# A gated recurrence and a spatial-gating block on one core: the state's decay moved into its product, mixing cut into steps, and a new order of steps

## The chip, the cores and the metric

The kernel runs on one core of a Trainium2 chip. Times are device microseconds (us) of one execution, and the profile is one execution recorded by the hardware. TensorE (PE) does the products, PEld is its weight loading, VectorE (DVE), ScalarE (ACT) and GpSimd (POOL) do element-wise work, and SP, ACT and POOL issue transfers.

## What is computed

A matrix-valued recurrence over 768 steps (batch 4, 8 heads of width 40), whose output goes through a gated feed-forward block that mixes over the sequence:

```python
for t in range(S):                                  # attention part
    m_new = maximum(f[t] + m, i[t])
    C = exp(f[t] + m - m_new) * C + exp(i[t] - m_new) * outer(v[t], k[t])
    n = exp(f[t] + m - m_new) * n + exp(i[t] - m_new) * k[t];  m = m_new
    y[t] = sigmoid(o[t]) * (C @ q[t]) / maximum(abs(n . q[t]), 1)
h = relu(x @ w_in); u, v = h[:512], h[512:]         # x is y, 320 wide
v_s = w_spatial @ layernorm(v) + b_spatial          # mixes the 768 positions
out = (u * v_s) @ w_out
```

## The kernel before

**Blocks.** The sequence of each batch is cut into 6 blocks of 128 positions, each of two chunks of 64; 24 blocks n in all, block n being k = n mod 6 of batch b = n div 6. Inside a chunk the recurrence is a masked product; between chunks a state of 40 x 41 per head is carried.

**One attention block.** s (line 605): scores of the two chunks, one in the upper and one in the lower half of the rows. ex (line 608): one product of the tables AT and GM, which hold the gates' running sums, gives the exponents; W (ACT, line 623) is its exponential. In batch 0 a second product eb (line 618) with a table sel gives Eb, the decay along a chunk; in the other batches Eb is loaded. KS takes s times W (DVE, line 629) and q times Eb (POOL, line 637). kt (POOL, line 648) scales k by the last column of W. dc (lines 659, 661) is k times v of each chunk, 64 rows each, the first chunk in rows 0 to 63, the second in rows 64 to 127. The state of the second chunk is dc plus the first state times its decay (d1 line 677, c1 line 680), that of the next block again (d2 line 687, c2 line 690); a block with k = 0 only copies (line 672). The states lie in RH below or above the rows of v, so that pv (lines 702, 703) gives a chunk's own part and the state's part in one product: 104 rows for the first chunk (64 where k = 0, since there is no state yet), 128 for the second. Then den (line 714), two products on DVE (lines 720, 723), a transpose px (line 743), and the split of x into a high and a low part (xH, xL).

**The feed-forward part.** All products of it are done in three terms (high x high, high x low, low x high). Per batch: six V (line 796, tile pm), each followed by the norm on ACT, DVE and POOL (lines 803 to 836) which gives vH and vL; eight pairs of pu (line 856) and pb (lines 862 to 864). A pb is 18 products over all six blocks of V in one accumulation, so it waits for the last of them; then bias, gate and split (lines 873 to 883); six pc (lines 899 to 901) and the output.

**Weights.** They come as 64-bit numbers and are converted on chip in cvt (lines 442 to 490): one ACT step, four DVE steps, a copy to the high part, a subtraction and an addition, in two banks of PSUM. The rest rows of w_in (64 of 320) come as one transfer for both halves.

**The order.** A list written out by hand (ORDER) gives every step's place; each engine and each queue runs its steps in that order. TensorE works in order, and a step that waits holds up all behind it. The loads of blocks, weights and the gate rows of block 0 (GM, lines 414 to 421) go over SP's queue, constant tables over POOL's. PSUM has 8 banks (pool "bank"), and the list's order sets which step gets which.

Of the kernel before, what the change touches and what calls it, by code (L numbers as in the profile page):

```python
# [8 lines left out]
F32 = mybir.dt.float32  # L9
F32R = mybir.dt.float32r  # L10
I32 = mybir.dt.int32
U32 = mybir.dt.uint32
# [13 lines left out]
RW = 2 * VW + 2 * KW  # L26
# [4 lines left out]
NKS, NRH = 3, 3  # L31
DEC_POOL = (0,)
GATE_POOL = (1, 2)
# [17 lines left out]
class Task:  # L51
    def __init__(self, name, eng, cost, fn, mode, lock, size):
        self.name, self.eng, self.cost, self.fn, self.mode, self.lock, self.size = name, eng, cost, fn, mode, lock, size
        self.deps, self.succ, self.bufs = set(), [], []
        self.due = self.own = None

    def length(self):
        return self.cost + (2.0 + self.size / 200.0 if self.size else 0.0)


class Plan:
# [11 lines left out]
    def add(self, name, eng, cost, fn, r=(), w=(), mode="M", lock=False, size=0, due=None, after=(), hold=()):  # L73
        t = Task(name, eng, cost, fn, mode, lock, size)
        t.own = due
        t.deps.update(after)
        for write, group in ((False, r), (True, w)):
            for x in group:
                b, part = x if isinstance(x, tuple) else (x, None)
                for o, p, wr in b.seen:  # L80
                    if o is not t and (write or wr) and (p is None or part is None or p == part):
                        t.deps.add(o)
                if write:
                    b.seen = [s for s in b.seen if part is not None and s[1] != part]
                b.seen.append((t, part, write))
                if b.pool and b not in t.bufs:
                    t.bufs.append(b)
                    b.users += 1
# [3 lines left out]
        for o in t.deps:  # L92
            o.succ.append(t)
# [5 lines left out]
half_neg rhz0 ident i sel f warm qk0_0 cgm0 qk0_1 cat0 rh0_0 cgm1 rh0_1 rhz1 wir_ld wi0 wi10_ld wi11_ld m0 rst rh1_0 m1 ksz2 rh1_1 ksz0 fa1 qk1_0 fs1  # L99
rhz2 qk1_1 fa0 ksz1 g1 s0 cat1 fs0 gh1 g0 eg1 is0 as0 gh0 gl1 ah0 dg0 gl0 da0 dg1 al0 wg1 m2 dg2 da1 dg3 wg0 eg0 fa2 th0 fs2 wa0 g2 gm1 ex0 is1 ebm0  # L100
gh2 rh2_0 W0 gl2 rh2_1 Eb0 as1 ks0_0 ebm1 wir_1 ks0_1 kt0 ah1 wir_2 we1 q0_1 Eb1 dc0 wir_3 wi10_1 c1_0 al1 wir_h0 qk2_0 wi10_2 pv0 qk2_1 is2 wa1 wir_4
wir_h1 den0 d2_0 wir_h2 wi10_3 wi11_1 xm0 as2 wir_h3 wi11_2 ra01 wi11_3 wi10_h0 wi10_4 wi11_h0 wir_s0 q1_0 ah2 wi11_4 gm2 wg2 xg0 q1_1 eg2 wir_5 ex1
rh3_0 th1 rh3_1 wi10_5 s1 W1 al2 wi10_s0 gm3 px0 qk3_0 wir_s1 kt1 wa2 qk3_1 ex2 wi11_5 xh0 we0 xj0 W2 wi11_s0 dc1 th2 wi10_l0 kt2 s2 ra02 wir_l1 ebm2
wi11_l0 Eb2 c2_0 dc2 gm4 xl0 d1_1 th3 xk0 ks1_0 V00 q2_0 ks1_1 c1_1 ks2_0 d2_1 pv1 ks2_1 re00 q2_1 c2_1 sq00 ex3 bsp den1 ebm3 s3 xm1 W3 d1_2 qk5_0
xg1 Eb3 qk5_1 va00 wir_l0 px1 kt3 rh4_0 gm5 rh4_1 c1_2 q3_0 xh1 dc3 ks3_0 xj1 ks3_1 pv2 d2_2 xl1 xk1 ex4 den2 q3_1 ebm4 W4 V01 c2_2 xm2 wi00_ld Eb4
xg2 wi01_ld d1_3 qk4_0 qk4_1 po00 px2 c1_3 re01 rh5_0 pv3 d2_3 nb00 rh5_1 xh2 xj2 ra10 xl2 gm6 th4 kt4 s5 c2_3 sq01 den3 we2 d1_4 xm3 ws00_ld dc4 vh00
xg3 ws01_ld ex5 rh6_0 c1_4 vn00 ebm5 px3 xk2 rh6_1 d2_4 va01 W5 V02 ws02_ld Eb5 ws03_ld po01 c2_4 ws04_ld xh3 ks5_0 d1_5 xj3 ks5_1 wi00_1 q5_0 xl3
re02 xk3 wi00_2 V03 ra11 sq02 gm7 q4_0 nb01 wi00_3 wi01_1 va02 wi00_4 vh01 q4_1 s4 wi01_2 re03 wi01_3 sq03 q5_1 qk6_0 ks4_0 qk6_1 th5 ks4_1 eb6_0 vn01
kt5 qk7_0 va03 pv4 wi01_4 qk7_1 ws00_h po02 eb7_0 wi00_5 ws01_h eb7_1 po03 dc5 wi00_h0 den4 vl00 xm4 ex6 wi01_h0 c1_5 W6 xg4 pv5 vl01 nb02 rh7_0 nb03
vh02 wi01_5 rh7_1 px4 den5 vn02 kt6 ex7 xm5 xh4 xg5 vl02 dc6 xj4 xl4 vh03 xk4 px5 wi00_s0 vn03 V04 ws00_l xh5 ws01_l ws05_ld xj5 ws02_h xl5 vl03  # L110
# [42 lines left out]
def ordered(plan):  # L153
# [816 lines left out]
```

## Time and profile before

| | |
|---|---|
| runs (us) | 424.12, 420.58, 418.35 (median 420.58) |
| profiled execution: span (us) | 422.7 |
| TensorE busy | 369.7 us |
| DVE, ACT, POOL busy | 250.9, 152.5, 139.8 us |
| mean granted clock of TensorE | 0.927 |
| moved | 35.62 MB |

Busy time of TensorE is time in which some product is under way, and products overlap, so a busy share near 100% does not say that it runs at its best. The granted clock is a share of 2.4 GHz. In waits, the releaser is what ended an idle time.

### The profile page before, as it was taken

How to read it: one execution, taken by the hardware profiler on the slowest of the kernel's cores; microseconds unless marked ns; L12 is line 12 of the kernel's file. 1: busy time of each engine (PE TensorE's matmuls, PEld its weight loads, DVE VectorE, ACT ScalarE, POOL GpSimd, SP SyncE). 2: the span in 40 equal slices, each digit the busy share in tenths (PEclk: the TensorE clock that was granted, in tenths of full speed). 3: DMA queues.
4: the chain of work that ended last, by engine and by line, in shares of the span. 5: the costliest groups of instructions: out<-in, count | busy, mean ns of one | idle time of the engine just before them, and what ended most of it. 6: DMA issues, size and time to landing. Idle time of an engine off the chain costs nothing.

```text
span 422.7 us, 9190 instructions
## 1 busy us (share of the span) xinstructions
PE 369.7 (87%) x3654; PEld 335.1 (79%) x3654; DVE 250.9 (59%) x540; ACT 152.5 (36%) x363; POOL 139.8 (33%) x150
## 2 busy tenths in 40 slices
PE   2045996979969999989799989999799999999996
PEld 1023874768869998868699878998699998899995
DVE  6145979867998737569693574335952626434231
ACT  2044268646331205723501521156320408441212
POOL 8044578753350114546530313325440004230000
PEclk9999999677969999989779985999779999999999
DMA  9940569354820505326312073200210100000001
GB/s 166 227 116 12 133 202 223 118 139 118 213 75 18 158 30 143 102 79 154 101 46 73 7 185 92 85 16 24 72 47 2 33 16 2 33 16 2 16 33 47
DMA packets 17262, 35.62 MB, mean 84 GB/s; under 512 B 3960, under 2 KB 9196, under 8 KB 17220
## 3 DMA queue, kind: packets, MB, share of 16 engines
q1 hardware_dynamic: 12556, 29.72, 26.6%
q10 hardware_dynamic: 4136, 4.52, 3.3%
q0 software_dynamic: 528, 0.81, 1.2%
q8 instruction: 29, 0.48, 0.5%
q14 instruction: 13, 0.11, 0.1%
HBM read 30.59 MB, written 4.42 MB: 83 GB/s over the span
## 4 chain that ended last, share of the span: by engine, by line
PE 67%; DVE 14%; DMA 10%; issue 4%; ACT 3%; POOL 1%; SPq 1%; ACTq 0%; DVEq 0%; POOLq 0%
PE pu L856 9%; PE pb L862 8%; PE pb L863 8%; PE pb L864 8%; PE pm L796 7%; PE pv L702 5%; DMA QK<-in_qk 5%; PE s L605 5%; PE pv L703 4%; PE pc L899 3%; PE pc L901 3%; PE pc L900 2%; PE dc L659 2%; DMA RH<-in_vk 2%; DVE KS L629 2%
## 5 line engine op out<-in xcount | busy, mean ns | idle before, releaser
L637 POOL TENSOR_TENSOR KS<-QK,Eb 40x512 f32<-40x512 f32 x44 | 57.5, 1312 | 70.1 <-PE pv L703 32.8
L862 PE MATMUL pb<-wsH,vH 128*128 128x384 f32 x192 | 68.0, 354 | 3.9 <-DVE wo_r L468 3.9
L863 PE MATMUL pb<-wsL,vH 128*128 128x384 f32 x192 | 67.1, 350 | 0.0
L864 PE MATMUL pb<-wsH,vL 128*128 128x384 f32 x192 | 66.9, 349 | 0.0
L873 DVE TENSOR_TENSOR pb<-pb,bsp 128x384 f32<-128x384 f32 x32 | 18.1, 565 | 54.3 <-PE pb L864 54.3
L883 ACT CAST gt<-pb 128x384 fp32r<-128x384 f32 x32 | 15.4, 480 | 76.7 <-DVE pb L876 76.7
L703 PE MATMUL pv<-RH,KS 128*64 128x41 f32 x384 | 37.9, 254 | 5.1 <-DVE KS L629 3.2
L702 PE MATMUL pv<-RH,KS 104*64 104x41 f32 (+1 forms) x384 | 38.0, 253 | 4.7 <-DVE KS L629 3.0
L605 PE MATMUL s<-QK 40*64 40x64 f32 x768 | 34.3, 251 | 8.9 <-DMA QK<-in_qk 8.9
L862 PEld LDWEIGHTS pb<-wsH,vH 128*128 128x128 f32 x192 | 38.1, 198 | 4.4 <-DVE wo_r L468 4.2
L605 PEld LDWEIGHTS s<-QK 40*64 40x64 f32 x768 | 30.6, 162 | 13.5 <-DMA QK<-in_qk 9.2
L812 POOL TENSOR_TENSOR st<-st,half_neg 128x1 f32<-128x1 f32 x24 | 13.4, 560 | 82.0 <-DVE st L809 65.8
L702 PEld LDWEIGHTS pv<-RH,KS 104*64 104x64 f32 (+1 forms) x384 | 31.2, 158 | 10.9 <-POOL st L812 3.3
L836 POOL TENSOR_TENSOR vL<-v,vH 128x512 fp32r<-128x512 f32 x24 | 31.1, 1299 | 23.6 <-ACT vH L818 15.2
L863 PEld LDWEIGHTS pb<-wsL,vH 128*128 128x128 f32 x192 | 38.2, 199 | 0.0
L864 PEld LDWEIGHTS pb<-wsH,vL 128*128 128x128 f32 x192 | 38.0, 198 | 0.0
L703 PEld LDWEIGHTS pv<-RH,KS 128*64 128x64 f32 x384 | 31.2, 159 | 7.7 <-DVE KS L629 2.8
L629 DVE TENSOR_TENSOR KS<-s,W 64x512 f32<-64x512 f32 x48 | 32.9, 686 | 6.9 <-PE s L605 4.3
L648 POOL TENSOR_TENSOR RH<-RH,W 128x320 f32<-128x320 f32 x24 | 18.7, 781 | 49.0 <-ACT W L623 34.9
L856 PE MATMUL pu<-xH,wiH 128*128 128x384 f32 x96 | 33.1, 345 | 0.0
L856 PE MATMUL pu<-xH,wiL 128*128 128x384 f32 x96 | 32.6, 340 | 0.0
L796 PE MATMUL pm<-wiH,xH 128*128 128x512 f32 x72 | 31.5, 437 | 0.0
(117 smaller groups left out, 818.8 us busy)
## 6 DMA issues: line engine op xcount, KB each, us to landing
RH<-in_vk SPq DMA_DIRECT2D x48, 242.0 KB
QK<-in_qk SPq DMA_DIRECT2D x48, 160.0 KB
out<-o ACTq DMA_DIRECT2D x24, 160.0 KB
Eb<-scr_e SPq DMA_DIRECT2D x33, 80.0 KB
ws<-in_w_sp SPq DMA_DIRECT2D x12, 192.0 KB
wi_raw<-in_w_in SPq DMA_DIRECT2D x4, 512.0 KB
wo_raw<-in_w_out SPq DMA_DIRECT2D x4, 320.0 KB
wir_raw<-in_w_rem SPq DMA_DIRECT2D x1, 512.0 KB
```

What stands on the lines that cost most here:

```text
L605: self.nc.tensor.matmul(o[64 - p0:128 - p0, h], q[p0:p0 + D, 0, h], q[p0:p0 + D, 1, h], start=True, stop=True)
L629: self.nc.vector.tensor_tensor(out=KS.t[r, e], in0=st()[r], in1=self.T(W)[r], op=ALU.mult)
L637: self.nc.gpsimd.tensor_tensor(out=KS.t[r, e], in0=self.T(QK)[r, 1], in1=self.T(Eb)[r], op=ALU.mult)
L648: self.nc.gpsimd.tensor_tensor(out=kt, in0=kt, in1=self.T(W)[:, :, L - 1:L].broadcast_to([128, H, D]), op=ALU.mult)
L702: self.nc.tensor.matmul(o[0:64, h], ks[0:ke, 0, h], v0[0:ke, h], start=True, stop=True)
L703: self.nc.tensor.matmul(o[64:128, h], ks[:, 1, h], v1[:, h], start=True, stop=True)
L796: self.nc.tensor.matmul(pmt(), l, r, start=i == 0, stop=i == len(terms) - 1)
L836: self.nc.gpsimd.tensor_tensor(out=vl(), in0=vt(), in1=vh().bitcast(F32), op=ALU.subtract)
L856: self.nc.tensor.matmul(put(), w, x, start=i == 0, stop=i == len(terms) - 1)
L862: self.nc.tensor.matmul(pbt(), vH[:, cd], wh[:, s], start=s == 0, stop=False)
L863: self.nc.tensor.matmul(pbt(), vH[:, cd], wl[:, s], start=False, stop=False)
L864: self.nc.tensor.matmul(pbt(), vL[:, cd], wh[:, s], start=False, stop=s == NB - 1)
```

## The change

The state's decay moves into dc. The k part of RH gets, beside the 64 rows of k, 40 to 64 rows of an identity (eye); kt multiplies both at once by the last column of an exponent tile XY that now holds W and Eb side by side, so that the identity becomes diagonal rows with the decay on them. dc then has 104 or 128 rows (k and v in 64 of them, decay and old state in the rest) and gives the new state directly; four heads go to the lower and four to the upper half of the output. It is two steps now, dc_0 and dc_1, and each is followed by two copies (cc), on DVE or ACT, in place of products and additions. For k = 0 the state rows are set to zero (cz), and pv has 104 and 128 rows in every block. In batch 0 the decay comes from a second exponent product with a table ATX, in place of eb.

pb is cut into six steps of three products, one for each block of V, and pc into four, each its own entry in the list. The gate's product is written to u in SBUF, not back to the bank.

Constant tables come from one transfer (const) and are spread out on chip. A conversion of weights has one ACT and three DVE steps in an SBUF tile, a copy and a subtraction. The rest rows of w_in are loaded once per half and twice over (0.5 MB more).

The list is new: it names an engine for steps that can run on more than one (copies, products, transfers), and so moves 27 of the 48 q and 16 of the 24 kt steps to DVE, 20 of 32 gl steps to POOL, and transfers from SP to ACT and POOL. The limits that were built in for the old list (pv of block n-2 ahead of s of block n, and so on) are gone. There are two KS tiles instead of three.

```diff
-NKS, NRH = 3, 3
-POOLS = dict(bank=8, QK=2, Eb=2, big=5, xL=3, xH=3, W=2, tmp=2, x=2, v2=14, s15=4, den=2, st=3, raw=4, late=1)
+NKS, NRH, NXY, NGM = 2, 3, 2, 2
+POOLS = dict(bank=8, QK=2, KT=2, big=5, xL=3, xH=3, x=2, v2=14, s15=4, den=2, st=3, raw=3)
...
-half_neg rhz0 ident i sel f warm qk0_0 cgm0 qk0_1 cat0 rh0_0 cgm1 rh0_1 rhz1 wir_ld wi0 wi10_ld wi11_ld m0 rst rh1_0 m1 ksz2 rh1_1 ksz0 fa1 qk1_0 fs1
-rhz2 qk1_1 fa0 ksz1 g1 s0 cat1 fs0 gh1 g0 eg1 is0 as0 gh0 gl1 ah0 dg0 gl0 da0 dg1 al0 wg1 m2 dg2 da1 dg3 wg0 eg0 fa2 th0 fs2 wa0 g2 gm1 ex0 is1 ebm0
+i@SP axz1@DVE axz0 f@ACT const@ACT cz0 qk0_0 rst axe0 m0 qk0_1 fa0 qk1_1@POOL qk1_0@POOL s0 is0@POOL rh0_1 fs0@POOL m1 g0 as0 gh0 ah0 al0@POOL
+axe1@DVE gmh0 fa1 s1 fs1 da1@ACT wa0@ACT is1@POOL gl0 gmm0 dg0@POOL dg1@ACT g1 rhz1@DVE rh0_0 dg2@POOL dg3@ACT gh1@DVE ksz1 as1 da0 gmm1 gl1 ah1 m2
...
+nb01 vn01 wi02_ld vh01 ws11_ld den4 vl01 re02 vl00@DVE pb001_0 pb000_0 sq02 wi01_3 ws01_h@POOL xg4 wi02_1 ws01_l@POOL ws02_ld xm4 px4 pb003_0 pb001_1
...
-                self.nc.tensor.matmul(o[0:D, h], kt[0:64, h], v0[0:64, h], start=True, stop=True)
-                if not last:
-                    self.nc.tensor.matmul(o[64:64 + D, h], kt[64:128, h], v1[64:128, h], start=True, stop=True)
...
-            add(f"d1_{n}", de, dcost, dec1, r=[(RH, "c0"), (Eb, 1)], w=[t1], lock=True)
-            add(f"c1_{n}", "DVE", 0.42, st1, r=[dc, t1], w=[(RH, "c1")])
...
+        def ktm(e):
+            self.eng(e).tensor_tensor(out=ktt(), in0=self.rh_k(n), in1=xyt()[:, :, :, L - 1:L].broadcast_to([128, 2, H, D]), op=ALU.mult)
...
+        for e in range(1 if last else 2):
+            def dcm(q, e=e):
+                kt, v, o, K = ktt(), self.rh_v(n, e), dct(), (64 + D, 128)[e]
+                for h in range(4):
+                    for p0 in (0, 64):
+                        hh = h + p0 // 16
+                        self.nc.tensor.matmul(o[p0:p0 + D, e, h], kt[0:K, e, hh], v[0:K, hh], start=True, stop=True)
+            def put(q, g, e=e):
+                m = n + e
+                lo = 64 * e
+                self.copy(q, self.rh_v(m, 1 - e)[lo:lo + D, 4 * g:4 * g + 4], dct()[64 * g:64 * g + D, e])
...
-            ke = 64 if k == 0 else 64 + D
...
-                self.nc.tensor.matmul(o[0:64, h], ks[0:ke, 0, h], v0[0:ke, h], start=True, stop=True)
+                self.nc.tensor.matmul(o[0:64, h], ks[0:64 + D, 0, h], v0[0:64 + D, h], start=True, stop=True)
...
-        vs = [x for s in range(NB) for x in self.vn[b, s]]
-        self.pbt.append(add(f"pb{name}", "PE", 3.15, pbm, r=vs + [F(f"wsH{hf}"), F(f"wsL{hf}")], w=[pb], due=self.moe_due(b, "pb", i), hold=[gt]))
...
+        for s in range(NB):
+            add(f"pb{name}_{s}", "PE", lambda e, s=s: pbm(s), r=[*self.vn[b, s], (F(f"wsH{hf}"), s), (F(f"wsL{hf}"), s)], w=[pb])
```

The new conversion of weights, whose steps take the place of shift, sign, power, low, a subtraction and an addition:

```diff
+        add(name + "_1", "ACT", base, r=[rb], w=[y])
+        add(name + "_2", "DVE", shift, w=[y])
+        add(name + "_3", "DVE", sign, r=[rb], w=[y])
+        add(name + "_4", "DVE", tail, r=[rb], w=[y])
+        add(name + "_h", "ACT/POOL", lambda e: self.copy(e, H_(), yt().bitcast(F32)), r=[y], w=[(F(wbuf + "H"), part)])
+        add(name + "_l", "DVE/POOL", lambda e: self.eng(e).tensor_tensor(out=L_(), in0=yt().bitcast(F32), in1=H_().bitcast(F32), op=ALU.subtract),
```

## Rows read from the trace of the kernel before

**Rows 1.** The page, part 1: busy time, share, instructions of each engine.

```profile
PE 369.7 (87%) x3654; PEld 335.1 (79%) x3654; DVE 250.9 (59%) x540; ACT 152.5 (36%) x363; POOL 139.8 (33%) x150
```

**Rows 2.** Busy time by stretch: length, each engine, granted clock, transfer share, GB/s.

```profile
0.00:50.00 50.00, 19.99 (x234) 15.52 (x234) 27.04 (x52) 15.32 (x35) 20.20 (x33) 1.00 0.61 138
50.00:130.00 80.00, 68.92 (x830) 58.37 (x829) 67.53 (x148) 41.68 (x97) 45.94 (x45) 0.85 0.53 144
130.00:410.00 280.00, 272.01 (x2543) 253.22 (x2542) 154.08 (x338) 93.08 (x227) 73.61 (x73) 0.93 0.21 60
410.00:422.70 12.70, 8.79 (x54) 8.00 (x52) 2.25 (x4) 2.42 (x6) 0.00 (x0) 1.00 0.11 39
```

**Rows 3.** Waits of PE: who waited for whom, us, times, longest.

```profile
PE ex L608 <- DMA GM<-gp: 14.8, 1, 14.8
PE s L605 <- DMA QK<-in_qk: 8.9, 3, 5.0
PE ex L608 <- issue: 5.2, 1, 5.2
```

**Rows 4.** Busy time by stretch again: the wait at the start, and around pv18.

```profile
10.00:24.00 14.00, 0.00 (x0) 0.00 (x0) 2.57 (x4) 0.54 (x3) 0.00 (x0) 1.00 0.81 196
249.40:263.00 13.60, 13.33 (x134) 11.65 (x135) 5.84 (x15) 1.55 (x3) 3.32 (x4) 0.52 0.37 104
```

**Rows 5.** Timeline of SP: start, us, engine, line, what it issues.

```profile
12.79 10.29 SPq L418 DMA_DIRECT2D GM<-gp  x4
```

**Rows 6.** Timeline of PE, start of the kernel: start, us, line, tiles, shapes.

```profile
24.71 0.77 PE L608 MATMUL ex<-GM,AT 84*128 84x512 f32 x1 [14.80 <-DMA GM<-gp]
...
41.36 0.76 PE L608 MATMUL ex<-GM,AT 84*128 84x512 f32 x1 [5.23 <-issue]
```

**Rows 7.** Chain of work that ended last, in order of time: the first V.

```profile
50.01 2.96 PE pm L796 x8
```

**Rows 8.** Timeline of PE, 52 to 57 us: a pv of blocks after the first, and dc.

```profile
52.90 0.25 PE L702 MATMUL pv<-RH,KS 104*64 104x41 f32 x1
...
53.80 0.23 PE L702 MATMUL pv<-RH,KS 104*64 104x41 f32 x1
...
53.96 0.51 PE L608 MATMUL ex<-GM,AT 84*128 84x512 f32 x1
...
56.30 0.23 PE L659 MATMUL dc<-RH 64*40 64x41 f32 x1
...
56.91 0.20 PE L659 MATMUL dc<-RH 64*40 64x41 f32 x1
```

**Rows 9.** Timeline of PE: pv of the first block, batch 2 and batch 3.

```profile
181.41 0.31 PE L703 MATMUL pv<-RH,KS 128*64 128x41 f32 x2 [1.08 <-DVE RH L672]
...
184.74 0.31 PE L703 MATMUL pv<-RH,KS 128*64 128x41 f32 x2
...
255.14 0.43 PE L703 MATMUL pv<-RH,KS 128*64 128x41 f32 x2
...
260.23 0.43 PE L703 MATMUL pv<-RH,KS 128*64 128x41 f32 x2
```

**Rows 10.** Groups of instructions, DVE and POOL: count, busy us, mean ns, idle before.

```profile
L637 POOL TENSOR_TENSOR KS<-QK,Eb 40x512 f32<-40x512 f32 x44 | 57.5, 1312 | 70.1 <-PE pv L703 32.8 <-DMA QK<-in_qk 28.6 <-DMA out<-o 2.9
L690 DVE TENSOR_TENSOR RH<-dc,tb 40x328 f32<-40x328 f32 x20 | 10.1, 503 | 0.9 <-POOL tb L687 0.4
L687 DVE TENSOR_TENSOR tb<-RH,Eb 40x328 f32<-40x328 f32 x15 | 11.6, 776 | 0.4
L459 DVE TENSOR_SCALAR wi_b<-wi_x 128x512 int32<-128x512 int32 x4 | 2.7, 685 | 0.0
```

**Rows 11.** Transfers by issue: queue, count, KB, us from issue to landing.

```profile
AT<-in_at POOLq DMA_DIRECT2D x2, 204.0 KB, 8.6
...
sel<-in_sel POOLq DMA_DIRECT2D x1, 42.0 KB, 4.3
```

More of the change, by code (lines that the diff above doesn't have):

```diff
@@ L51, with __init__ @@
 class Task:
[L52 to L58, printed above, removed]
+    def __init__(self, name, engs, fn, size):
+        self.name, self.engs, self.eng, self.fn, self.size = name, engs, engs[0], fn, size
+        self.deps, self.bufs, self.acc = set(), [], []
 class Plan:
@@ L71, in keep, with add @@
         return self.fixed[name]
-    def add(self, name, eng, cost, fn, r=(), w=(), mode="M", lock=False, size=0, due=None, after=(), hold=()):
-        t = Task(name, eng, cost, fn, mode, lock, size)
-        t.own = due
+    def add(self, name, engs, fn, r=(), w=(), size=0, after=(), hold=()):
+        t = Task(name, engs.split("/"), fn, size)
         t.deps.update(after)
@@ L239, in dma, with eng, copy @@
         return {"SP": self.nc.sync, "ACT": self.nc.scalar, "POOL": self.nc.gpsimd}[q].dma_start
+    def eng(self, e):
+        return {"DVE": self.nc.vector, "POOL": self.nc.gpsimd, "ACT": self.nc.scalar}[e]
+    def copy(self, e, out, in_):
+        if e == "ACT":
+            self.nc.scalar.copy(out=out, in_=in_)
+        else:
+            self.eng(e).tensor_copy(out=out, in_=in_)
     def add(self, *args, **kw):
@@ L320, in gates, with eye @@
+            def eye(e, half, rh=rh):
+                r, o = (slice(L, 128), K0) if half == 0 else (slice(0, L), K1)
+                self.copy(e, rh.t[r, o:o + KW].rearrange("p (h d) -> p h d", h=H), C()[r, r.start:r.start + D].unsqueeze(1).broadcast_to([L, H, D]))
+            for half in range(2):
+                add(f"eye{j}_{half}", "POOL/DVE/ACT", lambda e, half=half, eye=eye: eye(e, half), r=[F("const")], w=[(rh, ("eye", half))])
     def gates(self):
@@ L543, in load_ws, with lo @@
-        add(f"ws{q}{c}_h", "ACT", 0.51, hi, r=[t], w=[(F(f"wsH{q}"), c)], after=after)
-        add(f"ws{q}{c}_l", "DVE", 0.56, lo, r=[t, (F(f"wsH{q}"), c)], w=[(F(f"wsL{q}"), c)], lock=True)
+            self.copy(e, F(f"wsH{q}").t[:, c], tt())
+        def lo(e):
+            self.eng(e).tensor_tensor(out=F(f"wsL{q}").t[:, c], in0=tt(), in1=F(f"wsH{q}").t[:, c].bitcast(F32), op=ALU.subtract)
+        add(f"ws{q}{c}_ld", "SP/ACT/POOL", lambda e: self.dma(e)(out=tt(), in_=self.a["w_sp"][c][:, r]), w=[t], size=192)
@@ L597, in attention, with ld_e @@
-        s, ex = new("bank", "s"), new("bank", "ex")
+            add(f"gm{n}", Q, ld_g, r=[(F("scr_g"), z)], w=gparts, size=8)
+        if b:
+            for e, p0 in ((0, 64), (1, 0)):
+                def ld_e(q, e=e, p0=p0):
+                    self.dma(q)(out=XY.t[p0:p0 + D, e], in_=self.scr_e[2 * k + e, b * H:(b + 1) * H].unsqueeze(0).broadcast_to([D, H, L]))
+                add(f"eb{n}_{e}", Q, ld_e, r=[(F("scr_e"), z)], w=[(XY, ("b", e))], size=80)
+        if first:
+            add(f"cz{n}", "POOL/DVE", lambda e: self.eng(e).memset(RH.t[64:128, V0:V0 + VW], 0.0), w=[(RH, ("c0", 0)), (RH, ("c0", 1))])
@@ L683, in attention @@
[L683 to L692 removed]
+        add(f"th{n}", "ACT", tanh, w=[(RH, ("o", 0)), (RH, ("o", 1))])
@@ L839, in b_u @@
+        add(f"vl{name}", "POOL/DVE", lambda e: self.eng(e).tensor_tensor(out=vl(), in0=vt(), in1=vh().bitcast(F32), op=ALU.subtract), r=[v, vH], w=[vL])
     def b_u(self, b, hf, d):
@@ L886, in c_out @@
+        add(f"gl{name}", "DVE/POOL", lambda e: self.eng(e).tensor_tensor(out=gL(), in0=ut(), in1=gH().bitcast(F32), op=ALU.subtract),
+            r=[u, (gt, 0)], w=[(gt, 1)])
     def c_out(self, b, k):
```

841 lines of the change are left out of this document (383 added, 458 removed).

## The prediction

> **What bounds the kernel now.** The page's totals come first: TensorE is busy 87% of the span, no other engine over 59% [rows 1]. The question is therefore what TensorE's own time is made of, and that is read from three stretches and the tail [rows 2]. Up to 50 us it is busy for 20 of 50. From 50 to 130 it idles 80 - 68.9 = 11.1 us at a mean granted clock of 0.85, from 130 to 410 it idles 280 - 272.0 = 8.0 us at 0.93, and the last 12.7 us are nearly full. A granted clock below 1 is a mixture of the two levels, 1.2 and 2.4 GHz. Time lost to it, as length times (1 - clock): 80 x 0.15 = 12.0 us and 280 x 0.07 = 19.6 us. So the loss has three parts: a start in which TensorE waits, idle time later, and stretches at 1.2 GHz.
>
> The waits of TensorE name the start [rows 3]: 14.8 us for the four small transfers of gate rows into GM, and 5.2 us ahead of the second exponent product. In those 24 us nothing computes and the transfer engines move 196 GB/s [rows 4]: SP's queue issues the four gate transfers from 12.79 to 23.08 us [rows 5], behind the megabyte and a half of weights that it has issued before. TensorE's first product of block 0 that needs the gates stands at 24.71, the second block's at 41.36 [rows 6], and the first product of V (line 796, pm) at 50.01 [rows 7].
>
> Last, the products pv (lines 702 and 703). In 20 of the 24 blocks both halves use the full row height (104 or 128 rows), and a whole pv takes from 52.90 to 53.96, 1.06 us [rows 8]. In the first block of each batch line 702 takes 64 rows and line 703 takes 128, in turn, and each change of height costs a full stop: steps of (184.74 - 181.41) / 14 = 0.238 us at the full clock, 0.363 us at the low one [rows 9], against (53.80 - 52.90) / 15 = 0.060 for a pair of products in [rows 8]. Sixteen steps make 3.8 or 5.8 us. pv18 lies in a stretch of 13.6 us at a granted clock of 0.52 [rows 4], so TensorE ran at 1.2 GHz there; pv6 shows the same long steps.
>
> **The change, part by part.** Base is the profiled span of 422.7 us; the median of the runs, 420.58, is 2.1 lower, and I take that off at the end.
>
> *Start: -20 (-12 to -25).* The constants of 0.8 MB on POOL's queue go; one table of 108 KB and copies on chip replace them. The weights' loads stand behind the gate transfers, and these are spread over POOL's and ACT's queues. Ahead of them are then some 1.2 MB: at 196 GB/s 6 us, so the first exponent product should stand at 11 to 14 us instead of 24.71. The 5.2 us wait follows from the slow pv0 (DVE and ACT stand behind it in order), which becomes an ordinary pv. V of block 0 now needs 5.1 MB (four blocks' inputs, 0.8 MB each, gates, table, three weight pieces of 0.5 MB): 26 us at 196 GB/s from 2.5 us on, and four conversion steps of 0.685 [rows 10], so about 31 us instead of 50.01. TensorE has done about one attention block more by then, so 20 is taken, with 38 us and 27 us as the bounds for V.
>
> *First block of each batch: -12.2.* The state rows of block 0 are zeroed, and pv is 104 and 128 rows high everywhere. pv0 is in the term above. pv6 and pv18 (low clock) go from 5.8 to 1.06, pv12 (full clock) from 3.8 to 1.06: 4.7 + 4.7 + 2.7. If the low clock stays, 1.06 is 2.1 and the term 10.
>
> *50 to 130 us: -10.5 (0 to -21).* Here DVE is busy 67.5 of 80 us [rows 2] and TensorE waits for it. Of its work the decay goes: 20 + 20 additions of 0.50 and 15 + 15 products of up to 0.78 [rows 10], about 40 us in all, replaced by 88 copies of half the size, 39 of them on DVE. A weight conversion has four DVE steps instead of six. Against that 27 of POOL's q products (1.31 us each there), 16 kt and 13 vl come to DVE, while 20 gl, 10 xm and half of the wsL steps leave it: DVE's total stays near 240 us, but less falls into this stretch. And mixing (pb) no longer waits for all six blocks of V: it is cut in 6 steps of three products, and in the new order its first step stands after the fourth V, not after the sixth. That is what can fill the holes. What there is to win is 11.1 us idle and 12.0 - 2.0 us of low clock (2.0 is in pv6 already). I take half, since TensorE works in order and a fixed list can fill a hole only where the listed work is ready.
>
> *130 to 410 us: -12.8 (0 to -25.6).* Same reasoning: 8.0 idle and 19.6 - 2.0 low clock, half of it. The tail of 12.7 us ends in the same chain and is costed at nothing: the list after the last mixing step is as long as before.
>
> *The price: +9 (+3 to +14).* dc becomes 104 or 128 rows high. Its pairs now step by (56.91 - 56.30) / 15 = 0.041 us with 64-row halves side by side; pv's pairs, full height, by 0.060 [rows 8]. 44 new half products of 8 pairs make 352 pairs; between 0 and 0.019 each, 0 to 7 us. I take 5, nearer to pv, which has the same height and the same two column halves. The Trainium skill, "TensorE: Matmul & The Clock Gate", section "The mechanism", says that a weight load runs under a product in flight only when their row groups differ; that speaks against full-height packs, and by it dc would step wholly like pv: the sum would be 2 us longer. The two steps of [rows 8] agree with it in direction. Also, dc is now two separate stretches, and each change of tile shape costs (from the last pair of pv at 53.80 to the product at 53.96, 0.16 instead of 0.06) about 0.1 us on either side: 20 more stretches, 4 us; none if they stand beside a pv.
>
> dc also joins the recurrence: the next dc waits for the copies of the last. Reading the new order, I added up the TensorE work listed between each dc and the next: in 39 of 40 cases it is over 0.8 us, which is what a copy (half of 0.503) with two hand-overs should take. So it is costed at nothing; without the cover it would be 40 x 0.8 = 32 us.
>
> The sum: 422.7 - 20 - 12.2 - 10.5 - 12.8 + 9 = 376.2 us, 374 as the runs are counted. Its own range is 360 to 388.
>
> **Rivals.** *The new order fills everything.* Then the other halves, 10.5 + 12.8, go too: 353 of span, 351. For it: pb is 100 us of work that can stand anywhere. Against it: the clock falls after short waits, and some will stay.
>
> *Finer mixing fills nothing.* Up to six of the eight banks of PSUM are held by open pb sums while V and attention need the rest, so TensorE waits for a bank where it waited for DVE. Only start, pv and the price count: 422.7 - 20 - 12.2 + 9 = 399.5, 397; with the price at its upper end 402.
>
> *The recurrence through TensorE shows.* 376.2 + 32 = 408, 406, if ACT or DVE reach the copies late behind their other work.
>
> *Slower: block inputs land late on POOL's queue.* 28 of the 96 block inputs, and many small ones, move from SP to POOL, where a transfer is issued in order behind vector work. The one of 42 KB there took 4.3 us to land, those of 204 KB 8.6 [rows 11]; and the three longest waits for inputs on SP made 8.9 us [rows 3]. If every block waited 2.3 us, the 24 blocks would eat the 46.5 + 8.4 us between my sum and slower by 2%; at 2.5 us the time is 376 + 60 = 436, 434. Against it: the list asks for inputs one to two blocks ahead, some 10 us.
>
> **How the numbers follow.** Forecast 0.60, everything filled 0.10, nothing filled 0.18, recurrence 0.06, late inputs 0.06. A measurement of this kernel can tell about 2% from no change, that is 412 and 429. Faster: 0.60 + 0.10 + 0.17 + 0.03 = 0.90. Same: 0.01 + 0.03 + 0.02 = 0.06. Slower: 0.04. The range of 8 in 10 is 356 to 404: nearly all of the forecast's, half of the filled case near 353 left out, and most of the unfilled case in.
>
> **What would show it.** First exponent product at 11 to 14 us and V at about 31; all 24 pv at about 1.06 us; dc pairs between 0.041 and 0.060; idle from 50 us on about 10 us, and a granted clock of about 0.95. The forecast is wrong if V starts after 38 us, if TensorE's waits name copies into RH, banks or QK with over 20 us together, or if the clock stays at 0.9 although the mixed pv are gone.

## The result, and the profile after

The changed kernel takes 389.94 us (median of 4 runs, 387.61 to 390.9), the kernel before in the same job 420.89: a ratio of 0.924, 95% interval 0.918 to 0.931. That is faster by 31 us, where 46.5 were forecast, inside the range given (356 to 404) and 16 us above the forecast of 374. The profiled execution has a span of 388.3 us, 34.4 less than the 422.7 of before; the parts below are counted from these two traces and add up to this difference.

The page's part 1 answers to [rows 1]:

```profile
PE 350.1 (90%) x3654; PEld 312.1 (80%) x3654; DVE 250.1 (64%) x523; ACT 175.7 (45%) x395; POOL 164.4 (42%) x198
```

As many products as before, and VectorE as busy as before (250.1 against 250.9 us), in a shorter span. The stretches, as in [rows 2] (length, busy time of each engine, granted clock, transfer share, GB/s):

```profile
0.00:50.00 50.00, 31.22 (x397) 24.52 (x398) 40.18 (x78) 24.18 (x52) 28.21 (x42) 1.00 0.60 161
50.00:130.00 80.00, 70.78 (x661) 62.26 (x657) 64.67 (x119) 38.66 (x87) 42.45 (x50) 0.94 0.43 113
130.00:375.00 245.00, 238.81 (x2551) 216.30 (x2548) 142.70 (x323) 109.33 (x250) 91.58 (x105) 1.00 0.27 72
375.00:388.30 13.30, 9.27 (x62) 9.01 (x60) 2.56 (x5) 3.52 (x8) 2.12 (x3) 1.00 0.21 74
```

The granted clock reads 1.00 in the first row only because the trace has no clock record before 47.93 us (51.96 us in the trace of before); that TensorE runs at its lower level of 1.2 GHz there is read from its products: one of V's takes 441 ns there and 245 later.

In the start TensorE's idle time fell from 30.0 to 50 - 31.2 = 18.8 us. From 50 to 130 it hardly fell (11.1 to 9.2), but the clock rose from 0.85 to 0.94; from 130 us on the idle time is as it was (6.2 of 245 us), and the clock is 1.00. TensorE's waits, as in [rows 3] (us in total, times, longest):

```profile
PE s L591 <- DMA QK<-in_qk: 7.2, 3, 4.7
PE dc L649 <- issue: 4.7, 4, 2.7
PE ex L601 <- ACT ATX L265: 4.6, 2, 4.1
PE dc L649 <- DVE KT L636: 3.5, 3, 2.5
...
PE dc L649 <- ACT RH L265: 0.8, 1, 0.8
```

The 14.8 us for the gate rows and the 5.2 us ahead of the second exponent product are gone. What took their place in part is a wait of ex for ScalarE's copies into ATX, and dc for kt. The recurrence, the last row, costs 0.8 us in all; "issue" is time for which the profile names no releaser, so a part of those 4.7 us could belong to it too.

**Where the time went, counted by products.** From the starts of all records of TensorE's products: a product's time is the time from its start to the next one's, less idle time in between. "Cold" is everything up to the first rise of the clock, some 50 us into either trace; "slow" is later time at 1.2 GHz. The 5 us ahead of the first product and the 4 us behind the last are left out.

```
us                                   before   after
idle, cold part                        25.0    14.1
idle, later                            19.5    15.4
products, cold part                    22.1    29.3
products, later, slow                  60.6     8.9
products, later, at 2.4 GHz           286.7   311.7
all products of pv                     45.6    28.1
all others than pv, slow               43.2     8.7
one product at 2.4 GHz, ns: pb          176     184
                            pc          154     160
                            pu          178     183
                            pm          241     245
                            dc         24.0    26.7
```

Three gains and one price stand in it. Idle time: -15.0 us, 10.9 of them in the start. pv: -17.5. The slow products other than pv: at the full clock's rates the 43.2 us of before would be 24.0 and the 8.7 of after 4.7, so 19.2 - 4.0 = 15.2 us were regained. Against them, nearly every product got dearer: 576 x 8.9 ns for pb, 288 x 6.2 for pc, 256 x 4.7 for pu, 192 x 4.0 for pm and 704 x 2.7 for dc make 5.1 + 1.8 + 1.2 + 0.8 + 1.9 = 10.8 us. These are means: most products of pb take 175 ns in both kernels, and the price stands in a few that take far longer. In the changed kernel 48 of the 562 products of pb at 2.4 GHz take 28 to 163 ns more than 175, which is the 5.1 us; 42 of the 48 stand beside a change to another tile or a wait.

### The profile page after: what moved, and what is told of

The parts are those of the page before. It is cut to its first block, busy times and chain, and to the rows that moved or that the text cites. A ratio compares the mean times of both kernels' runs of the same rounds, so it can differ in the third digit from the quotient of the medians.

```text
span 388.3 us, 9200 instructions
## 1 busy us (share of the span) xinstructions
PE 350.1 (90%) x3654; PEld 312.1 (80%) x3654; DVE 250.1 (64%) x523; ACT 175.7 (45%) x395; POOL 164.4 (42%) x198
## 4 chain that ended last, share of the span: by engine, by line
PE 61%; DVE 18%; issue 6%; POOL 6%; DMA 5%; ACT 3%; ACTq 1%; DVEq 0%; POOLq 0%
PE pu L802 10%; PE pm L750 7%; PE pb L807 7%; PE pb L809 6%; PE pb L808 6%; PE pv L668 4%; PE dc L649 4%; PE pc L832 3%; PE s L591 3%; DVE KS L625 3%; PE pc L834 3%; PE pc L833 3%; PE px L708 2%; DMA scr_a<-ap 2%; DVE v L774 1%
## 5 line engine op out<-in xcount | busy, mean ns | idle before, releaser
L809 PEld LDWEIGHTS pb<-wsH,vL 128*128 128x128 f32 x192 | 36.7, 191 | 3.9 <-POOL vL L783 2.4
L807 PEld LDWEIGHTS pb<-wsH,vH 128*128 128x128 f32 x192 | 36.7, 191 | 3.2 <-ACT vH L772 1.0
L591 PE MATMUL s<-QK 40*64 40x64 f32 x768 | 29.6, 236 | 8.6 <-DMA QK<-in_qk 7.2
L649 PEld LDWEIGHTS dc<-RH,KT 104*40 104x40 f32 (+1 forms) x704 | 19.3, 128 | 22.1 <-issue 11.6
L591 PEld LDWEIGHTS s<-QK 40*64 40x64 f32 x768 | 27.0, 149 | 11.1 <-DMA QK<-in_qk 7.5
L818 POOL TENSOR_TENSOR gt<-u,gt 128x384 fp32r<-128x384 f32 x20 | 20.8, 1044 | 35.3 <-ACT gt L817 34.1
L649 PE MATMUL dc<-RH,KT 104*40 104x41 f32 (+1 forms) x704 | 24.5, 217 | 10.2 <-issue 4.7
L620 DVE TENSOR_TENSOR KS<-s,XY 64x512 f32<-64x512 f32 x48 | 32.7, 686 | 1.5 <-PE s L591 0.5
L772 ACT ACTIVATE vH<-pm,st 128x512 fp32r<-128x512 f32 x24 | 18.6, 776 | 31.7 <-DVE v L774 16.2
L812 ACT ACTIVATE u<-pu 128x384 f32<-128x384 f32 x32 | 15.7, 490 | 36.8 <-PE pu L802 32.6
L625 POOL TENSOR_TENSOR KS<-QK,XY 40x512 f32<-40x512 f32 x21 | 29.3, 1395 | 6.4 <-DMA XY<-scr_e 4.3
L832 PE MATMUL pc<-woH,gt 128*128 128x320 f32 x96 | 31.7, 330 | 0.0
L834 PE MATMUL pc<-woH,gt 128*128 128x320 f32 x96 | 29.8, 310 | 0.9 <-DVE gt L818 0.9
L815 DVE TENSOR_TENSOR pb<-pb,bsp 128x384 f32<-128x384 f32 x32 | 17.8, 561 | 19.2 <-PE pb L809 19.0
```

Source lines behind the costliest of these rows:

```text
L591: self.nc.tensor.matmul(o[64 - p0:128 - p0, h], q[p0:p0 + D, 0, h], q[p0:p0 + D, 1, h], start=True, stop=True)
L620: self.nc.vector.tensor_tensor(out=KS.t[r, e], in0=st()[r], in1=xyt()[r, e], op=ALU.mult)
L625: self.eng(q).tensor_tensor(out=KS.t[r, e], in0=self.T(QK)[r, 1], in1=xyt()[r, e], op=ALU.mult)
L649: self.nc.tensor.matmul(o[p0:p0 + D, e, h], kt[0:K, e, hh], v[0:K, hh], start=True, stop=True)
L807: self.nc.tensor.matmul(pbt(), vH[:, cd], wh[:, s], start=s == 0, stop=False)
L809: self.nc.tensor.matmul(pbt(), vL[:, cd], wh[:, s], start=False, stop=s == NB - 1)
```

## The experiments

Theory: the gain is the sum of three parts, of which pv and the clock came as forecast, and the start fell short, since VectorE's work stands ahead of V there. The rivals are that the price of dc or of finer steps ate it, that the cold clock did, or that a transfer is late. Ratios are to the kernel before on the same chip; the changed kernel's 389.94 us comes from another job, so a difference of 2 or 3 us from it is at the edge of what these runs can tell.

Each run has one trace, and the start varies from one to the next. In the changed kernel's own trace the first exponent product stands at 15.71 us and V at 45.40. In three runs below that leave the start as it is (pv the other way, mixing whole, dc with 64 rows) they stand at 13.68, 13.08 and 13.59, and at 45.77, 43.36 and 44.07. So a V that is 2 us earlier shows nothing by itself.

**pv alone (before, with pv at full height).** The kernel before, its state rows of block 0 zeroed and pv 104 and 128 rows high in every block:

```diff
-            ke = 64 if k == 0 else 64 + D
+            ke = 64 + D
...
+            add(f"cz{n}", "POOL", 0.4, lambda: self.nc.gpsimd.memset(RH.t[64:128, 0:VW], 0.0), w=[(RH, "c0")])
```

> The kernel before with one thing of the change: pv is 104 and 128 rows high in the first block of each batch too (the state rows and the q rows are zeroed). If the change of height inside pv costs what rows 9 show and stands on the path: pv0, pv6, pv12 and pv18 go from 3.8 to 5.8 us to about 1.1 (2.1 at the low clock), and the kernel is 12 to 16 us faster, 405 to 409 us. Rival: other work (DVE in batch 0, inputs in the later batches) is late behind them anyway, and the kernel gains under 5 us, 416 or more.

407.36 us (406.18 to 409.66), ratio 0.968 (0.961 to 0.974): about 14 us less. By products pv falls from 45.6 to 33.7 us. The wait for the gate rows stays (13.5 us), so this gain is pv's own. The 5.2 us ahead of the second exponent product stay too (5.23, put down to VectorE here), although pv of block 0 now takes 2.3 us instead of 5.9. So the prediction's reading that this wait follows from the slow pv of block 0 does not hold.

**pv alone, the other way (after, with pv 64 rows high in the first blocks).**

```diff
-                self.nc.tensor.matmul(o[0:64, h], ks[0:64 + D, 0, h], v0[0:64 + D, h], start=True, stop=True)
+                self.nc.tensor.matmul(o[0:64, h], ks[0:ke, 0, h], v0[0:ke, h], start=True, stop=True)
```

> The changed kernel with one thing undone: pv of the first block of each batch has 64 and 128 rows in turn again. If the height is worth what the prediction says, 12 to 16 us come back: 402 to 406 us, with steps of 0.24 to 0.36 us in those pv. Rival: in the new order the time of these pv is covered by waits that are there anyway: under 4 us, 390 to 394.

404.22 us (401.94 to 408.66), ratio 0.959 (0.952 to 0.966), that is 14 to 15 us above the changed kernel. The timeline of TensorE, first and last rows of pv of block 6, in the changed kernel and then here:

```profile
120.42 0.25 PE L668 MATMUL pv<-RH,KS 104*64 104x41 f32 x1
...
121.32 0.23 PE L669 MATMUL pv<-RH,KS 128*64 128x41 f32 x1
```

```profile
123.34 0.31 PE L669 MATMUL pv<-RH,KS 64*64 64x41 f32 x2
...
126.90 0.31 PE L670 MATMUL pv<-RH,KS 128*64 128x41 f32 x2
```

Taken away or put back, the turns of 64 and 128 rows in pv are worth 14 us. The clock tells a second thing. In this run products are slow for 21.6 us after the first rise, in the run before it for 46.5; 60.6 before and 8.9 after. So the slow stretches go mostly with the new list and its steps, and only in part with pv.

**Mixing whole again (after).** The six steps of each pb stand together where the last stood:

```diff
-... pb001_0 pb000_0 sq02 ... pb003_0 pb001_1 ... vl05 pu010 pb001_5 pb002_5 g001 ...
+... sq02 ... vl05 pu010 pb001_0 pb001_1 pb001_2 pb001_3 pb001_4 pb001_5 pb002_0 ...
```

> The changed kernel with the six steps of each mixing product put together again, at the place of the last one in the list. If mixing in steps is what fills the holes after 50 us, V's chain is bare again and the kernel is 8 to 15 us slower, 398 to 405 us, with idle time of TensorE beside V and a lower granted clock. Rival: the steps fill nothing that matters, and the rest of the new order does it: 388 to 393 us.

439.8 us (437.92 to 441.31), ratio 1.045 (1.039 to 1.052): 50 us above the changed kernel, and slower than the kernel before. That is far outside both expectations. Its busy time by stretch and its waits:

```profile
60.00:80.00 20.00, 7.80 (x61) 5.17 (x59) 18.75 (x35) 10.75 (x25) 14.06 (x15) 0.67 0.21 60
180.00:200.00 20.00, 12.59 (x49) 10.34 (x50) 7.08 (x18) 8.84 (x17) 8.66 (x11) 0.83 0.26 67
360.00:380.00 20.00, 12.67 (x114) 10.21 (x114) 12.80 (x32) 8.20 (x19) 5.07 (x7) 0.74 0.00 1
```

```profile
PE px L708 <- DVE x L690: 10.2, 6, 3.6
...
PE pm L750 <- ACT xH L717: 6.6, 5, 3.1
PE pv L668 <- DVE KS L625: 5.6, 1, 5.6
```

There is a hole wherever V is made, since the steps of pb that stood between the V are gone and TensorE waits for the other engines' copies; and where it idles, the clock falls (0.67 at 7.8 us busy of 20). By products, 61 us are idle against 29.5, and 39.4 slow against 8.9. This says what the steps of pb do in the changed kernel: they are the filler that keeps TensorE and its clock up. It does not say what they would bring to the old list, because the new list was made around them.

**The start: the gate rows ahead of the weights (before).** The three loads of weights go behind the last gate transfer on SP:

```diff
-... rhz1 wir_ld wi0 wi10_ld wi11_ld m0 rst ... dg2 da1 dg3 wg0 ...
+... rhz1 wi0 m0 rst ... dg2 da1 dg3 wir_ld wi10_ld wi11_ld wg0 ...
```

> The kernel before with three tokens of its list moved: the first three weight loads (1.5 MB) are issued on SP's queue behind the four gate transfers. If transfers set the start, the first exponent product comes at 12 to 15 us instead of 24.7 and the kernel is 6 to 12 us faster, 409 to 415 us. Rival: what follows on DVE (weight conversions) sets the first V, whose weights now land later: V stays at about 50 us and the time within 2 us of 420.9.

419.74 us (414.0 to 422.37), ratio 0.994 (0.987 to 1.000): 0 to 6 us. Its timeline of TensorE:

```profile
18.70 0.77 PE L608 MATMUL ex<-GM,AT 84*128 84x512 f32 x1 [9.40 <-DMA GM<-gp]
38.01 0.77 PE L608 MATMUL ex<-GM,AT 84*128 84x512 f32 x1 [5.23 <-issue]
...
45.37 0.51 PE L796 MATMUL pm<-wiH,xH 128*128 128x512 f32 x1
```

The first exponent product comes 6 us earlier than in [rows 6] and V 4.6 us earlier than in [rows 7], but the time falls by some 3, between the two expectations. The interval leaves open whether all of the 4.6 us came through or none.

**The start: VectorE's conversions left out (after).**

```diff
-        add(name + "_2", "DVE", shift, w=[y])
-        add(name + "_3", "DVE", sign, r=[rb], w=[y])
-        add(name + "_4", "DVE", tail, r=[rb], w=[y])
+        if not name.startswith("wi1"):
+            (the three lines, one level deeper)
```

> The changed kernel without the three DVE steps of each of the first three weight conversions (nine steps of 512 columns, 7.8 us of DVE between 18 and 45 us; the weights of V are then not the reference's). If DVE sets the first V, V comes 5 to 8 us earlier than 45.5 and the kernel is 4 to 8 us faster, 382 to 386 us. Rival, transfers: the third weight piece lands at 30 us in any case and the attention chain in front of V sets the rest; V moves by under 2 us and the time stays at 388 to 391.

387.04 us (386.12 to 388.78), ratio 0.916 (0.910 to 0.921): some 3 us less than the changed kernel, between the two expectations, and at the edge of the runs' scatter (387.61 to 390.9 there). VectorE has 22.8 us of work between 18 and 45 us instead of 25.8, and V starts at 41.32 instead of 45.40.

**The start: TensorE kept warm (after).** 98 dummy products of 320 columns between the first blocks' products:

```diff
+                for _ in range(reps):
+                    self.nc.tensor.matmul(self.T(wb)[:, 0:DM], w[:, 0:128], w, start=True, stop=True)
```

> The changed kernel with 19 groups of products that nobody reads (98 products of 320 columns on ones), put where TensorE waits or runs at 1.2 GHz before the first V. If the low clock of the first 45 us is what the start costs, the attention products there take half the time, V comes 4 us or more earlier and the kernel is 4 to 8 us faster, 382 to 386. Rival, DVE sets the first V: the products run at the full clock, but V stays within 1.5 us of 45.5 and the time at 388 to 391; where the groups are in the way it is a little slower.

388.77 us (387.5 to 394.05), ratio 0.918 (0.912 to 0.924). The products of the start now run at the full clock from the first block on (30 ex take 8.5 us instead of 12.5), V stands at 43.85, and it brings 1 to 2 us at most, which the intervals don't tell from none. The cold clock alone is not what holds the start.

**The price of dc: 64 rows (after).** The two halves of dc still stand apart, each over 64 rows:

```diff
-                kt, v, o, K = ktt(), self.rh_v(n, e), dct(), (64 + D, 128)[e]
+                kt, v, o, K = ktt(), self.rh_v(n, e), dct(), slice(64 * e, 64 * e + 64)
...
-                        self.nc.tensor.matmul(o[p0:p0 + D, e, h], kt[0:K, e, hh], v[0:K, hh], start=True, stop=True)
+                        self.nc.tensor.matmul(o[p0:p0 + D, e, h], kt[K, e, hh], v[K, hh], start=True, stop=True)
```

> The changed kernel with dc over its 64 rows of k and v alone; the part with the diagonal rows and the old state is left out, so the state is that of the last chunk. If height is what dc pays (5 us in the prediction's sum), its pairs go from about 0.05 to about 0.041 us and the kernel is 2 to 6 us faster, 384 to 388. Rival: dc is paid by its own stretches and waits, not by its height: under 2 us, 388 to 391.

389.33 us (388.4 to 392.18), ratio 0.922 (0.916 to 0.928): no difference. Busy time of dc alone between 130 and 375 us, first in the changed kernel, then here:

```profile
130.00:375.00 245.00, 14.74 (x464) 11.45 (x464) 8.09 (x25) 9.55 (x33) 1.00 0.27 72
```

```profile
130.00:375.00 245.00, 14.78 (x464) 11.39 (x464) 8.08 (x25) 9.56 (x33) 1.00 0.26 72
```

464 products take 14.7 us at 104 and 128 rows and 14.8 us at 64. The height costs nothing. Where dc's 2.7 ns a product (1.9 us in all) go is seen in the starts of its records. Inside a stretch products follow one another by 20.5 ns at either height, and by 19.8 in those stretches of the kernel before that nothing interrupts, where the upper and the lower 64 rows took turns; a pair takes 0.041 us, as in [rows 8]. That is 0.5 us in all. The rest stands at the ends of stretches: from the last product of a stretch to the next tile's first are 120 ns on average, where before it was 50.

By the rule named in the prediction (the Trainium skill, "TensorE: Matmul & The Clock Gate", section "The mechanism": a weight load runs under a product in flight only when their row groups differ) dc, whose stretches now use the same rows throughout, would step like pv, at 0.060 a pair. The trace doesn't bear this out: 0.041. The comparison with pv passed over that pv's weights have 64 columns and dc's 40 [rows 8]; no run varies that.

**The start: lighter VectorE and earlier exponents (after).** Three memsets and one copy leave VectorE, and the identity copies of ATX move ahead of the wait in ScalarE's list:

```diff
-... gmm1 gl1 ah1 m2 gmh1@POOL al1 wi12_ld axi0 wa1@ACT axi1 eye0_0@ACT rhz0@DVE ... eye2_0@DVE ...
+... axi0 axi1 gmm1 gl1 ah1 m2 gmh1@POOL al1 wi12_ld wa1@ACT eye0_0@ACT rhz0 ... eye2_0@ACT ...
```

> The changed kernel with six tokens of its list altered: the two identity copies into ATX go ahead of the copy that waits for a transfer on ACT, one identity copy into RH goes from DVE to ACT (1.28 us on DVE) and three zeroings of RH from DVE to POOL (0.33 us each). If the first exponent product waits for that copy and DVE sets V, the product comes 1 to 2 us earlier, V 2 to 3 us, and the kernel gains 2 to 3 us: 387 to 388. Rival: POOL and ACT are late in turn, and nothing moves or V comes later: 390 to 392.

389.25 us (387.63 to 389.4), ratio 0.919 (0.913 to 0.925): no difference to be told. The first exponent product stands at 14.46 and V at 43.35, which is no earlier than in runs that leave the start alone (13.08 and 43.36).

**The start: the third piece of weights early (after).**

```diff
-... wi11_ld ksz0 ra011 ... kt1@DVE xg0 wi10_ld@POOL wi12_3 ...
+... wi11_ld wi10_ld ksz0 ra011 ... kt1@DVE xg0 wi12_3 ...
```

> One edit in the changed kernel: the load of the third piece of V's weights is issued on SP right behind the second (about 11 us) instead of on POOL at 24.7 us, where it landed at about 30. Theory (VectorE's list sets V's start: it is busy 18.3 to 45.4 without a hole, so a piece that lies ready earlier still waits in that list): V starts at 44 to 46 us, the ratio to before stays at 0.920 to 0.928. Rival (the late piece sets V's start): V starts at 38 to 41 us and the kernel gains 4 to 7 us, ratio 0.908 to 0.915.

390.54 us (389.61 to 391.33), ratio 0.930 (0.922 to 0.938), V at 44.89. No gain, as the theory had it: the late piece is not what V waits for.

**The start: three edits together (after).** The warm TensorE, the lighter VectorE and the early piece in one kernel.

> Three edits of the start together, the whole computation kept: the third weight piece early as in the run beside it, 98 dummy products that keep TensorE at 2.4 GHz, and four small tasks moved off VectorE with the exponent table's identity copies ahead. Alone the last two brought about 2 us and nothing. Theory (VectorE's list is the limit, none of the three takes much from it): V at 42 to 45 us, ratio 0.912 to 0.921. Rival (several limits lie close together, each edit alone only uncovers the next): more than the sum of the parts, V at 38 us or earlier, ratio 0.90 to 0.91.

389.82 us (387.61 to 394.7), ratio 0.926 (0.917 to 0.935). V stands at 47.30, later than either theory had it: the clock fell back to 1.2 GHz between 18 and 45 us (granted 0.87) in spite of the dummies. Nothing adds up to a gain.

**The same, without the nine conversion steps (after).**

> The three edits of the run beside it, and the nine bit assembly steps of V's first weights left out (the products then read weights that are not assembled), which takes 7.8 us off VectorE's list ahead of V. Theory (VectorE's list is the limit): V 5 to 8 us earlier than in the run beside it, at 36 to 39 us, ratio 0.900 to 0.912. Rival (the inputs' transfers or the attention chain of the first blocks take over): V not before 40 us, ratio within 0.005 of the run without the nine steps alone, 0.911 to 0.921.

386.72 us (385.61 to 389.21), ratio 0.922 (0.913 to 0.931), V at 42.91. Against the run with three edits, in the same job, the nine steps are worth 4.4 us of V and 3.1 us of time, much as in the run that leaves them out of the changed kernel. VectorE has 20.3 us of work between 18 and 45 us, so it is no longer full, and V does not come at 36 to 39 us. The theory in the strict form, that VectorE's list alone sets V, falls: after some 4 us something else holds it. TensorE is busy for 26.3 of these 27 us, but with the dummies in it, so this run can't say whether it is the blocks' chain through four engines or the dummies themselves. That stays open.

**V ahead of block 2 (after).** V of block 0 and all that it needs go ahead of block 2's attention in the list, on VectorE and on TensorE:

```diff
-... pv1 wi10_1 eye2_1 wi11_3 ... kt2@DVE ... dc2_0 xg1 ... pv2 ... wi12_4 ... xl0 ... wi12_l ... dc3_0 ... V00 ...
+... pv1 eye2_1 ... wi10_1 wi11_3 ... wi12_4 xh0 wi12_h xl0 xk0 wi12_l kt2@DVE ... dc2_0 V00 xg1 ... pv2 ... dc3_0 ...
```

> An edit of the list alone, the work stays whole: V of block 0 and what it needs (the rest of the conversions, px of block 0, its copies) stand ahead of block 2's attention on VectorE and on TensorE, where in the changed kernel V stands behind pv of blocks 0, 1 and 2; the third weight piece is issued on SP behind the second. Theory (V's late start is the place that the list gives it, behind three blocks of attention that go through a VectorE with no hole, and what costs time there is VectorE's whole work in the start, not V's place in it): V at 35 to 40 us, pv of block 2 as much later, the time within 2 us of the changed kernel, ratio 0.919 to 0.929. Rival (V's start itself sets the time, as the prediction's term had it: 1 us earlier is about 0.7 us less): 5 to 8 us earlier gives 4 to 6 us, ratio 0.910 to 0.915.

393.43 us (393.15 to 395.56), ratio 0.937 (0.928 to 0.947). The timeline of TensorE, pv of block 1, V and pv of block 2:

```profile
30.52 0.31 PE L668 MATMUL pv<-RH,KS 104*64 104x41 f32 x1
...
41.35 0.80 PE L750 MATMUL pm<-wiH,xH 128*128 128x512 f32 x1
...
46.23 0.22 PE L668 MATMUL pv<-RH,KS 104*64 104x41 f32 x1
```

V is 4 us earlier than in the changed kernel, pv of block 2 5 us later (41.26 there), and the kernel is, if anything, 3 us slower, which neither expectation had. The run that left conversions out had V just as early (41.32), pv of block 2 also 4 us earlier (37.19), and was 3 us faster. So an earlier V that is paid for with a later block 2 is worth nothing here, and V's start, with which the prediction measured the start, is a poor measure. The only edit of the start that shows a gain is the one that takes work off VectorE, some 3 us both times, each at the edge of the runs' scatter.

No version tried beats the changed kernel by a margin that its whole computation and the intervals bear out.

## Why the prediction was right or wrong

The forecast of faster was right, with the parts in their places and one of them twice too large. Term by term, in us, the measured side from the table of products:

```
                                forecast   measured
start, with pv of block 0          -20       -11.0
pv of blocks 6, 12, 18             -12.2     -11.8
pv of the other 20 blocks            0        -1.6
50 us to the end, idle and clock   -23.3     -19.3
price                               +9       +10.8
not in the sum (eb, ex, px, s)       0        -1.6
                                   -46.5     -34.5
```

The measured start is the idle time of the cold part (-10.9), pv of block 0 (5.9 to 1.8, -4.1) and 4.0 us more that the low clock cost the other cold products: those other than pv took 16.2 us where the full clock's rates give 8.9, and now 23.8 for 12.5. The last row but the sum is eb, which is gone, 2.0 us at the full clock's rates, and small changes of ex, px and s.

**The start is the step that failed.** The prediction took V's start as the measure, put it at 31 us from "26 us at 196 GB/s from 2.5 us on, and four conversion steps of 0.685", and took 20 for it. V came at 45.40, beyond the 38 us at which the text called itself wrong. Two things are missing in the working. (A slip in its reading changes nothing: the wait in which TensorE does nothing is the 14 us from 10 to 24 us of [rows 4], not 24 us.) The transfers are not among them: the third weight piece, issued at 24.7 us, landed at about 30, where 28.5 had been worked out, and issuing it earlier brought nothing. First, V's place in the list: in the old one a single pv stands ahead of it on TensorE, in the new one three do. The new kernel's timeline:

```profile
23.54 0.31 PE L668 MATMUL pv<-RH,KS 104*64 104x41 f32 x1
...
30.75 0.31 PE L668 MATMUL pv<-RH,KS 104*64 104x41 f32 x1
...
41.26 0.31 PE L668 MATMUL pv<-RH,KS 104*64 104x41 f32 x1
...
45.40 0.80 PE L750 MATMUL pm<-wiH,xH 128*128 128x512 f32 x1
```

The blocks go by at 7.2 and 10.5 us each. "About one attention block more" was two: by 45 us the old kernel had done one pv and no V, the new one three pv. Second, VectorE's queue, which the prediction read from 50 us on but not before. The stretch from 18 to 45 us (busy time of TensorE, weight loads, VectorE, ScalarE, GpSimd, then clock and transfers), and VectorE's costliest groups in it (count, busy us, mean ns, idle ahead):

```profile
18.00:45.00 27.00, 20.26 (x281) 16.35 (x283) 25.82 (x47) 14.47 (x32) 16.91 (x18) 1.00 0.63 171
```

```profile
L620 DVE TENSOR_TENSOR KS<-s,XY 64x512 f32<-64x512 f32 x7 | 4.8, 685 | 0.2
L636 DVE TENSOR_TENSOR KT<-RH,XY 128x640 f32<-128x640 f32 x4 | 3.8, 958 | 0.0
L488 DVE SCALAR_TENSOR_TENSOR wi_y<-wi_raw,wi_y 128x512 int32<-128x512 int32 x3 | 3.5, 1170 | 0.1
L625 DVE TENSOR_TENSOR KS<-QK,XY 40x512 f32<-40x512 f32 x3 | 2.5, 831 | 0.1
L482 DVE TENSOR_SCALAR wi_y<-wi_y 128x512 int32<-128x512 int32 x3 | 2.2, 739 | 0.1
L485 DVE SCALAR_TENSOR_TENSOR wi_y<-wi_raw,wi_y 128x512 int32<-128x512 int32 x3 | 2.1, 687 | 0.0
```

There is next to no idle time ahead of any: VectorE is busy for 25.8 of 27 us. The start went from waiting for transfers to a VectorE that is full. The three pieces' conversions are 7.8 us of that, not four steps of 0.685. That VectorE's work costs some 3 us there is what the two runs without those steps show; what lies under it is open. The chain of work that ended last gives a hint: from 25.7 to 36.7 us it runs mainly over VectorE, and from 37.96 us to V over TensorE's own products of px, s, dc, pv and ex, at the low clock. The first exponent product came at 15.71, after 11 to 14, in this trace; with the same start it came at 13.1 to 13.7 in three others, so this reading of the prediction was right within the scatter.

**pv: right.** 11.8 by products for blocks 6, 12 and 18, where 12.2 were forecast, and 4.1 for block 0; the two runs that move all four alone show 14 and 14 to 15.

**The fill: near in size, wrong in kind.** The prediction took half of the idle time and half of the slow clock. In fact almost none of the idle time was filled (4.1 us of 19.5) and nearly all of the slow clock went, from 60.6 us of slow products to 8.9; that these two come to 19.3, near the 23.3 forecast, is in part luck. The waits that remained no longer cost the clock. The run with mixing whole shows the steps of pb at work there, and the rival "finer mixing fills nothing" falls with it.

**The price: right as a sum, by luck.** 10.8 against 9. The 5 us for dc's height were nothing: inside its stretches dc pays 0.5 us, and not for its height. What is paid is changes of tile, which the prediction priced at 4 us for dc alone: dc's ends make the rest of its 1.9 us, and pb pays 5.1 us in 48 single products. The cut into steps of three accounts for only a part of those: with mixing whole again 23 such products and 2.9 us are left.

**The recurrence and the late inputs.** The recurrence was costed at nothing, and next to nothing it was: 0.8 us of waits are put down to the copies into RH. The inputs on POOL's queue did not come late either; the issues of after:

```profile
RH<-in_vk POOLq DMA_DIRECT2D x14, 242.0 KB, 3.7
...
QK<-in_qk POOLq DMA_DIRECT2D x14, 160.0 KB, 3.4
```

They land in 3.4 to 3.7 us, where I had bounded by 4.3 and 8.6 from [rows 11], which were read in the start with all queues full.

## What to carry to other kernels

When a wait for transfers is taken away at the start of a kernel, ask which engine is full next, with every step that stands ahead of the one you care about in that engine's list, and count the steps that the new list puts ahead of it on TensorE. Don't measure a start by the moment at which one stage begins: two kernels here have the same V within 0.05 us and differ by some 6 us, one of them with less work for VectorE. Read such a moment from several traces: here it moves by 2 us in kernels whose start is the same. A filler in small steps is worth more than the idle time it takes, if it keeps the clock up; here its products got 5% dearer, about 2% of it by the cut into steps.

## What the runs showed of the hardware

**Tile height alone is free, turns of 64 and 128 rows are not.** dc at 104 and 128 rows and at 64 rows takes the same time (14.7 and 14.8 us for 464 products). pv that takes turns of 64 and 128 rows steps by 0.238 us, where a pair of 104 and 128 rows, which also take turns, takes 0.060 [rows 8, 9].

**VectorE slowed beside GpSimd.** The same conversion step takes 0.69, 1.10 or 1.72 us in the start. The timeline, VectorE's steps and, below, GpSimd's:

```profile
38.49 1.39 DVE L620 TENSOR_TENSOR KS<-s,XY 64x512 f32<-64x512 f32 x2
39.80 1.72 DVE L488 SCALAR_TENSOR_TENSOR wi_y<-wi_raw,wi_y 128x512 int32<-128x512 int32 x1
```

```profile
38.46 1.28 POOL L625 TENSOR_TENSOR KS<-QK,XY 40x512 f32<-40x512 f32 x1
39.70 1.27 POOL L496 TENSOR_TENSOR wiL<-wi_y,wiH 128x512 fp32r<-128x512 f32 x1
```

The conversion, begun at 39.80 while GpSimd works until 40.97, ends at 41.52: 0.55 us after GpSimd, close to its own 0.69. The one of 1.10 us also began beside a GpSimd step and ended 0.55 us after it. The two products of L620, beside a GpSimd step of the same kind, take their usual 0.69 each. The Trainium skill, "SBUF — State Buffer", section "SBUF: two separate sides", has it that VectorE and GpSimd share a pair of ports as an exclusive lock, which a VectorE step with two inputs in SBUF needs only against a GpSimd step that reads SBUF; L620 reads one of its two from PSUM. The two rows agree; no run here took the GpSimd step away, so as a cause it is argued and not shown.
